# The first loads of q and k, issued ahead of the opening barrier

## The chip, the core and the metric

The kernel runs on one core of a Trainium2 chip. The core has a TensorE (PE), a VectorE (DVE), a ScalarE (ACT), a GpSimd (POOL) and a SyncE (SP), and 16 DMA engines that move data for all of them. SyncE, ScalarE and GpSimd each issue DMA loads into a queue of their own; the queues meet on the same 16 DMA engines. In this text "engine" alone is one of the five, and "DMA engine" is one of the 16.

The metric is the device time of one execution, in microseconds (us). A profile is one traced execution; its span is 1.3 to 1.9 us shorter than the device time of the same execution, so spans are compared with spans and times with times.

## The reference, cut to what matters

```python
# q, k, v: 4 x 6400 x 256 f32; moe_A 8x256x16, moe_B 8x16x256, w_gate 256x8
qn = q / norm(q, axis=1); kn = k / norm(k, axis=1)
a = softmax(kn.T @ qn / tau)             # 256 x 256 for each of 4 batches
x = (v @ a).reshape(25600, 256)
# x + a mixture of 8 low-rank adapters (rank 16), the 2 best of 8 for each row
```

Nothing can be computed before the first rows of q and k are on the chip, and the 256 x 256 product of a batch needs all of that batch's q and k.

## The kernel before: the parts that the change touches

The inputs are f32 in DRAM. Nearly all loads are issued by GpSimd, whose queue casts f32 to bf16 on the way. Only the first 2 of the first batch's 50 row groups of q and k come uncast, over SyncE and ScalarE, and ScalarE casts them; three small MoE loads follow on the same two queues.

```python
def load_consts():                        # called after the first two loads
    ...
    nc.sync.dma_start(W["A0"], ...)       # 128 KB, rows of 512 B
    nc.scalar.dma_start(W["B0"], ...)     # 128 KB, rows of 1 KB
    nc.scalar.dma_start(W["wg0"], ...)    # 8 KB

def do_load(s, what, b, i, c, n):
    ...
        if (b, c) == (0, 0):
            ...
            (nc.sync if what == "q" else nc.scalar).dma_start(W[what], src[b, :, 0:n, :])  # 256 KB each
            return
    nc.gpsimd.dma_start(t[:, c - c0:c - c0 + n, :], src[b, :, c:c + n, :])                  # casts

for s in steps:                           # a static order for all five engines
    do[s.key[0]](s, *s.key[1:])
    if s.key[0] == "load":
        n_load += 1
        if n_load == 2:
            load_consts()
        if n_load == 4:
            make_consts()                 # identity matrix on GpSimd, and others
```

The framework puts an opening barrier ahead of all this. In the built program each of the four other engines executes a DRAIN that counts its arrival up, and then waits for a release. GpSimd writes four small constants, executes a DRAIN, waits until four have arrived, and releases them.

## Time and profile before

| | before |
|---|---|
| device time, 3 runs | 256.03 us median (255.64 to 256.05) |
| span of the profile | 254.1 us |
| busy share: PE, DVE, ACT, POOL | 85%, 75%, 66%, 12% |
| GpSimd's queue (q0), share of 16 DMA engines' span | 74.8% |
| SyncE's queue (q1), share of 16 DMA engines' span | 25.7% |

First from the page of before: the rows of DMA activity in 40 slices of the span (a digit is the busy share in tenths), and the DMA queues with packets, MB and their share of 16 DMA engines' time.

```profile
DMA  7999999999999999999999999999999999999994
...
q0 software_dynamic: 7488, 39.06, 74.8%
q1 hardware_dynamic: 3968, 26.61, 25.7%
q10 hardware_dynamic: 336, 0.40, 0.6%
```

Only the first and the last slice leave the DMA engines time. So the DMA engines are read as the bound, and what is to be had at the start is their idle time. (The page's chain that ended last lies 49% on PE and 39% on DMA, so this reading rests on the DMA row and not on that chain.) The next view is the table of stretches for before: the stretch in us, its length, the busy time of the five engines, the granted clock, the DMA share (over 1 where packets overlap) and GB/s.

```profile
1.00:1.50 0.50, 0.00 (x0) 0.00 (x0) 0.29 (x3) 0.00 (x0) 0.26 (x1) 1.00 0.00 0
1.50:2.00 0.50, 0.00 (x0) 0.00 (x0) 0.00 (x0) 0.00 (x0) 0.50 (x2) 1.00 0.63 66
2.00:2.50 0.50, 0.00 (x0) 0.00 (x0) 0.00 (x0) 0.35 (x1) 0.50 (x2) 1.00 0.86 115
...
4.50:5.00 0.50, 0.00 (x0) 0.00 (x0) 0.00 (x0) 0.38 (x1) 0.50 (x2) 1.00 1.60 306
```

No byte moves before 1.5 us. The timeline of before shows what the engines do meanwhile: start and length in us, engine (SPq, ACTq: the issue of a load), line, operation, tiles, and in brackets the idle time before it and what ended it.

```profile
0.74 0.40 ACTq L540 DMA_DIRECT2D y<-in_k_dram  x1
0.75 0.38 SPq L540 DMA_DIRECT2D y<-in_q_dram  x1
...
1.24 0.66 POOL L542 DMA_DIRECT2D qk<-in_q_dram  x1 [0.79 <-POOLq L925]
...
4.62 1.14 ACT L737 CAST qk<-y 128x512 bf16<-128x512 f32 x2 [0.97 <-DMA y<-in_q_dram]
...
14.72 0.39 PE L557 MATMUL acc_107<-qk 128*128 128x256 bf16 x1 [7.88 <-DMA qk<-in_k_dram]
```

SyncE and ScalarE issue their loads at 0.75 us, as soon as the barrier opens. PE computes on these first rows at 5.8 us and then waits 7.9 us, until 14.72 us, for GpSimd's first k load. So the early rows do not shorten PE's wait themselves; what counts is when GpSimd's stream runs.

### The profile page before, as it was taken

How to read it: one execution, taken by the hardware profiler on the slowest of the kernel's cores; microseconds unless marked ns; L12 is line 12 of the kernel's file. 1: busy time of each engine (PE TensorE's matmuls, PEld its weight loads, DVE VectorE, ACT ScalarE, POOL GpSimd, SP SyncE). 2: the span in 40 equal slices, each digit the busy share in tenths (PEclk: the TensorE clock that was granted, in tenths of full speed). 3: DMA queues.
4: the chain of work that ended last, by engine and by line, in shares of the span. 5: the costliest groups of instructions: out<-in, count | busy, mean ns of one | idle time of the engine just before them, and what ended most of it. 6: DMA issues, size and time to landing. Idle time of an engine off the chain costs nothing.

```text
span 254.1 us, 6344 instructions
## 1 busy us (share of the span) xinstructions
PE 216.1 (85%) x2643; PEld 192.7 (76%) x2643; DVE 190.0 (75%) x486; ACT 166.8 (66%) x270; POOL 30.1 (12%) x58
## 2 busy tenths in 40 slices
PE   0064993899999999999989999879999979999970
PEld 0053881588999996799779999769999869999860
DVE  0055589779889977898979995689888888888910
ACT  4344437558786767888758668453877869768770
POOL 7001220040020002000030100510000210000000
PEclk9999799799999999999999999999999999999997
DMA  7999999999999999999999999999999999999994
GB/s 186 218 215 210 210 221 211 211 220 218 211 219 208 316 299 290 259 213 224 208 214 218 221 212 216 213 208 347 282 282 320 332 323 313 319 421 426 426 411 189
DMA packets 11820, 66.47 MB, mean 262 GB/s; under 512 B 1424, under 2 KB 2320, under 8 KB 7184
## 3 DMA queue, kind: packets, MB, share of 16 engines
q0 software_dynamic: 7488, 39.06, 74.8%
q1 hardware_dynamic: 3968, 26.61, 25.7%
q10 hardware_dynamic: 336, 0.40, 0.6%
q8 instruction: 20, 0.33, 0.5%
q14 instruction: 8, 0.07, 0.1%
HBM read 78.91 MB, written 26.21 MB: 414 GB/s over the span
## 4 chain that ended last, share of the span: by engine, by line
PE 49%; DMA 39%; ACT 3%; DVE 3%; POOL 2%; issue 1%; ACTq 0%; POOLq 0%
DMA qk<-in_k_dram 22%; PE Y_ps L876 13%; DMA v<-in_v_dram 9%; DMA qk<-in_q_dram 8%; PE Y_ps L880 6%; PE T_ps L752 6%; PE ZL_ps L774 4%; PE gzT_ps L863 3%; PE Z_ps L843 2%; PE acc_417 L557 2%; PE acc_418 L557 2%; DVE a_bf L726 2%; PE acc_2620 L557 1%; PE acc_2621 L557 1%; ACT a_exp L678 1%
## 5 line engine op out<-in xcount | busy, mean ns | idle before, releaser
L585 DVE TENSOR_TENSOR ssq<-ssq,sq 128x1280 f32<-128x1280 f32 (+1 forms) x27 | 43.4, 1607 | 27.2 <-ACT sq L579 25.3
L876 PE MATMUL Y_ps<-a_bf,vT 128*128 128x256 bf16 x400 | 60.0, 273 | 0.0
L579 ACT ACTIVATE sq<-qk 128x1280 f32<-128x1280 bf16 (+1 forms) x27 | 36.8, 1364 | 26.5 <-DVE ssq L585 19.7
L732 ACT COPY y<-Y_ps 128x512 f32<-128x512 f32 x79 | 45.8, 587 | 12.3 <-PE Y_ps L880 9.8
L557 PEld LDWEIGHTS <-qk 128*128 128x128 bf16 x400 | 33.8, 103 | 24.5 <-DMA qk<-in_k_dram 16.0
L732 ACT COPY vT<-T_ps 128x1024 bf16<-128x1024 bf16 (+1 forms) x44 | 37.0, 871 | 6.7 <-PE T_ps L752 6.5
L876 PEld LDWEIGHTS <-vT 128*128 128x128 bf16 x400 | 37.6, 98 | 3.7
L880 PE MATMUL Y_ps<-ball,gzT 128*128 128x256 bf16 x200 | 38.2, 273 | 0.3 <-DVE gzT L734 0.3
L557 PE MATMUL acc_107<-qk 128*128 128x256 bf16 x50 | 15.2, 314 | 17.1 <-DMA qk<-in_k_dram 11.3
L542 POOL DMA_DIRECT2D v<-in_v_dram x20 | 12.2, 611 | 128.5 <-PE T_ps L752 80.8
L752 PE MATMUL T_ps<-ident,v 128*128 128x128 bf16 x400 | 27.1, 220 | 0.3 <-DMA v<-in_v_dram 0.3
L561 PEld LDWEIGHTS <-qk 128*128 128x128 bf16 x242 | 24.5, 101 | 3.6
L752 PEld LDWEIGHTS <-v 128*128 128x128 bf16 x400 | 23.9, 98 | 1.5 <-DMA v<-in_v_dram 1.2
L880 PEld LDWEIGHTS <-gzT 128*128 128x128 bf16 x200 | 19.4, 98 | 3.0 <-DVE gzT L734 0.6
L774 PE MATMUL ZL_ps<-waA_sb,vT 128*128 128x136 bf16 x280 | 19.7, 222 | 1.1 <-DVE waA_sb L720 0.9
L863 PE MATMUL gzT_ps<-ident,gz 128*128 128x128 bf16 x200 | 19.7, 219 | 0.3
L734 DVE COPY gzT<-gzT_ps 128x512 bf16<-128x512 bf16 (+1 forms) x39 | 15.0, 390 | 5.7 <-PE gzT_ps L863 5.0
L774 PEld LDWEIGHTS <-vT 128*128 128x128 bf16 x280 | 17.7, 98 | 1.8 <-issue 1.5
L579 ACT ACTIVATE ssq<-qk 128x1536 f32<-128x1536 bf16 x8 | 11.9, 1482 | 9.8 <-DMA qk<-in_k_dram 5.1
L734 DVE COPY y<-Y_ps 128x512 f32<-128x512 f32 x21 | 14.3, 690 | 3.3 <-PE Y_ps L880 3.2
L732 ACT COPY zl<-ZL_ps 128x272 f32<-128x272 f32 (+1 forms) x35 | 13.9, 447 | 3.4 <-PE ZL_ps L774 3.3
L566 PEld LDWEIGHTS <-qk 128*128 128x128 bf16 x168 | 15.2, 100 | 1.2 <-issue 0.2
(304 smaller groups left out, 441.7 us busy)
## 6 DMA issues: line engine op xcount, KB each, us to landing
out_dram<-y SPq DMA_DIRECT2D x18, 1280.0 KB, 18.0
v<-in_v_dram POOLq DMA_DIRECT2D x20, 640.0 KB, 20.5
qk<-in_q_dram POOLq DMA_DIRECT2D x7, 1088.0 KB, 24.1
qk<-in_k_dram POOLq DMA_DIRECT2D x7, 1088.0 KB, 29.0
qk<-in_q_dram POOLq DMA_DIRECT2D x2, 1024.0 KB, 18.8
qk<-in_k_dram POOLq DMA_DIRECT2D x2, 1024.0 KB, 23.2
out_dram<-y SPq DMA_DIRECT2D x4, 512.0 KB, 7.1
qk<-in_q_dram POOLq DMA_DIRECT2D x2, 512.0 KB, 17.3
```

The lines of the kernel that those rows point to most:

```text
L557: nc.tensor.matmul(acc[ic][:, 0:256], kt[:, j, ic * P:(ic + 1) * P], qt[:, j, :], start=c == 0, stop=False, skip_group_check=True)
L561: nc.tensor.matmul(acc[ic][:, 256:384], kt[:, j, ic * P:(ic + 1) * P], kt[:, j, ic * P:(ic + 1) * P], start=False, stop=False, skip_group_ ...
L566: nc.tensor.matmul(acc[ic][:, 384:512], qt[:, j, ic * P:(ic + 1) * P], qt[:, j, ic * P:(ic + 1) * P], start=False, stop=c == NC - 1, skip_ ...
L579: nc.scalar.activation(out[:, 0:n, :], t[:, j:j + n, :], ACT.Square)
L585: nc.vector.tensor_tensor(out=t, in0=t, in1=held["sq", (w, b, g), ""][:, 0:n, :], op=OP.add)
L732: nc.scalar.copy(out, in_)
L734: nc.vector.tensor_copy(out, in_)
L752: nc.tensor.matmul(ps[:, ic, j, :], vt[:, c + j, ic * P:(ic + 1) * P], W["ident"], is_transpose=True, start=(ic + j == 0), stop=(ic == CC ...
L774: nc.tensor.matmul(ps[:, j, :], vT[:, ic, c + j, :], st[b]["waA"][:, ic, :], start=(j == 0 and ic == 0), stop=(j == n - 1 and ic == CC - 1 ...
L863: nc.tensor.matmul(ps[:, j, :], gz[:, j, :], W["ident"], is_transpose=True, start=(j == 0), stop=(j == n - 1))
L876: nc.tensor.matmul(ps[:, j, :], vT[:, ic, c + j, :], st[b]["a"][:, ic, :], start=(j == 0 and ic == 0), stop=False, skip_group_check=True)
L880: nc.tensor.matmul(ps[:, j, :], gzT[:, c + j - UNITS[u][0], :], W["B"], start=False, stop=(j == 1), skip_group_check=True)
```

## The change

Its intent: SyncE and ScalarE have nothing to do while they wait at the barrier, so they issue their first loads ahead of it. GpSimd's loads stay behind it.

```diff
+def first_ahead(nc, names):
+    def move(nc):
+        main, body = nc.main_func.blocks[:2]
+        first = [i for i in body.instructions if i.name in names]
+        ...
+        at = next(n for n, i in enumerate(main.instructions) if type(i).__name__ == "InstMemset")
+        main.instructions = main.instructions[:at] + first + main.instructions[at:]
+        body.instructions = rest
+    nc.at_finalize(move)
 ...
-                (nc.sync if what == "q" else nc.scalar).dma_start(W[what], src[b, :, 0:n, :])
+                early.append((nc.sync if what == "q" else nc.scalar).dma_start(W[what], src[b, :, 0:n, :]))
 ...
+    early = []
 ...
+    first_ahead(nc, {i.ins.name for i in early})
```

In the built program the two loads now stand in front of their engine's DRAIN, that is, in front of its arrival at the barrier.

More of the change, by code (lines that the diff above doesn't have):

```diff
@@ L424 @@
         (2, 4), (3, 2), (3, 4)}
+def first_ahead(nc, names):
+    def move(nc):
+        main, body = nc.main_func.blocks[:2]
+        first = [i for i in body.instructions if i.name in names]
+        assert len(first) == len(names), (names, len(first))
+        rest = [i for i in body.instructions if i.name not in names]
+        at = next(n for n, i in enumerate(main.instructions) if type(i).__name__ == "InstMemset")
+        main.instructions = main.instructions[:at] + first + main.instructions[at:]
+        body.instructions = rest
+    nc.at_finalize(move)
 @with_exitstack
```

## The prediction

> **What bounds the kernel now.** The core's DMA engines. The page's DMA row reads 9 in all slices but the first and last. The table of stretches gives a DMA share of 1.04 for 2-220 us and 0.96 for 220-252 us, against PE busy 0.85 of the span. The only empty DMA time is the start: share 0.00 before 1.5 us, 0.63 in 1.5-2, 0.8 in 2-3.
>
> **What the change moves.** Two issues, q on SyncE (starts at 0.75 us, 0.38 us long) and k on ScalarE (0.74 us, 0.40 us), 256 KB each. Nothing is added or removed. In the trace SyncE arrives at the barrier at 0.00 us and ScalarE at 0.14 us, then both wait for GpSimd's release at 0.63 us. So q should start near 0.0 us and k near 0.14 us: 0.6 to 0.75 us earlier. The MoE loads after them move up by about 0.4 us.
>
> **Cost.** ScalarE reaches the barrier only after its issue: 0.14 plus the 0.43 us between two of its issues is 0.57 us. GpSimd now passes the gathering wait at 0.55 us, so the barrier may open 0.03 to 0.07 us later, and GpSimd's first load (1.24 us) with it.
>
> **How much is worth something.** The trace's DMA packets say that the first bytes of q and k move 1.0 us after issue (1.76 us), and that packets of SyncE's and ScalarE's queues fill the engines until about 5.0 us. GpSimd's queue starts its first packet at 4.35 us and is never empty again until 223 us. The Trainium skill, "DMA: Bandwidth & Descriptors", section "Issuing engines are not separate DMA queues", says that all issuers run on the same 16 engines and interleave; the trace agrees (share up to 1.60 where they overlap, 4.5-5 us). Two cases:
> - GpSimd's queue is held back until 4.35 us by the other queues' packets: it starts up to 0.65 us earlier, and everything shifts by that.
> - Its start is set by GpSimd's own issue: it stays at 4.35 us (or 4.40), but finds the engines nearly free. The other queues' packets after 4.35 us keep 16 engines busy for about 0.5 us (estimate from the packets); this is saved, less the later barrier.
>
> Either way 0.4 to 0.65 us. As the DMA engines never idle afterwards, most of it should reach the end. The earlier casts (ScalarE at 4.62 to about 4.0 us) and first four matmuls (5.81 to about 5.1 us) are worth nothing by themselves: PE then waits for a k load until 14.72 us.
>
> **Prediction.** 255.5 us, range 255.0 to 256.0, against 256.03 before (whose runs scatter by 0.4 us). Faster by over 2%: 0.01; within 2%: 0.98; slower by over 2%: 0.01.
>
> **What would show it.** Timeline: q and k issues before 0.2 us, ScalarE's casts at about 4.0 us, first matmul at about 5.1 us. Stretches: DMA share over 0.5 in 1.0-1.5 us, and below 1.3 in 4.5-5 us. GpSimd's first issue at 1.24 to 1.31 us; k landing that lets PE go on at 14.1 to 14.3 instead of 14.72 us; the same lead (0.3 to 0.7 us) at the last store.
>
> **What would make it wrong.** An issue ahead of the barrier takes longer there, and delays the barrier by more than 0.1 us; the reported time starts with the first issue instead of at a fixed point; DMA engines idle between the early loads and GpSimd's first packet; a matmul clock step (cold until 18.96 us) or a later collision of loads and stores that falls differently.

## The result, and the profile after

| | before | after |
|---|---|---|
| device time | 255.81 us median of 6 (255.64 to 256.05) | 255.69 us median of 6 (255.41 to 256.10) |
| ratio after/before | | 0.9994, 95% interval 0.9981 to 1.0007 |
| same kernel again, second set | 255.72 (11 runs) | 255.20 (6 runs), ratio 0.9978 (0.9963 to 0.9992) |
| same kernel again, third set | 255.84 (11 runs) | 255.52 (5 runs), ratio 0.9985 (0.9973 to 0.9997) |
| span of the first profile | 254.1 us | 254.3 us |

A ratio is the mean time of one kernel's runs over that of the other's of the same rounds, so it is not quite the ratio of the medians that stand beside it. The mean of the three ratios is 0.9986: about 0.36 us faster. The traces are not typical of this. The traced executions of the changed kernel were the slowest of its first set (256.10 us), the second slowest of six in the second (255.54 us) and the slowest of the third (255.75 us); of before, the first trace is of the fourth fastest of six (255.84 us), and that of a later repeat of the fastest of five (255.41 us). So the traced spans have the changed kernel 0.17 us slower on the mean (254.01 against 253.84 us), while the runs have it faster. Traces show where time goes; the gain is read from the runs.

In the DMA row of after's page one digit has changed, that of the first slice:

```profile
DMA  9999999999999999999999999999999999999994
...
q0 software_dynamic: 7488, 39.06, 74.9%
q1 hardware_dynamic: 3968, 26.61, 25.7%
q10 hardware_dynamic: 336, 0.40, 0.5%
```

The stretches of after:

```profile
1.00:1.50 0.50, 0.00 (x0) 0.00 (x0) 0.45 (x3) 0.00 (x0) 0.08 (x1) 1.00 1.24 135
1.50:2.00 0.50, 0.00 (x0) 0.00 (x0) 0.00 (x0) 0.19 (x1) 0.50 (x1) 1.00 0.42 123
2.00:2.50 0.50, 0.00 (x0) 0.00 (x0) 0.00 (x0) 0.50 (x1) 0.50 (x2) 1.00 0.99 381
...
4.50:5.00 0.50, 0.19 (x1) 0.13 (x2) 0.00 (x0) 0.26 (x1) 0.50 (x2) 1.00 0.68 139
```

And the timeline of after:

```profile
0.00 0.38 SPq L554 DMA_DIRECT2D y<-in_q_dram  x1
0.12 0.38 ACTq L554 DMA_DIRECT2D y<-in_k_dram  x1
...
1.42 0.66 POOL L556 DMA_DIRECT2D qk<-in_q_dram  x1 [0.97 <-POOLq L941]
...
3.21 0.60 ACT L751 CAST qk<-y 128x512 bf16<-128x512 f32 x1
4.14 0.62 ACT L751 CAST qk<-y 128x512 bf16<-128x512 f32 x1 [0.33 <-DMA y<-in_k_dram]
...
15.06 2.32 PE L571 MATMUL acc<-qk 128*128 128x256 bf16 x10 [9.21 <-DMA qk<-in_k_dram]
```

Everything early is earlier: the issues by 0.62 and 0.75 us, the data in 1.0 to 1.5 us, the first cast by 1.4 us. Then comes the surprise: PE goes on at 15.06 us instead of 14.72, that is 0.34 us *later*. A second trace of the unchanged kernel (r_before, below) shows how much of this is chance:

```profile
15.15 0.82 PE L557 MATMUL acc<-qk 128*128 128x256 bf16 x3 [7.96 <-DMA qk<-in_k_dram]
```

So before goes on at 14.72 or 15.15 us, and the changed kernel, in its three traces, at 15.06, 14.93 and 15.13 us. What is shown is that the early lead is missing at this point, not that the change makes it later.

To see why, one must look below the load. A load is complete when all 16 DMA engines have counted its semaphore up. The Trainium skill says so in "DMA: Bandwidth & Descriptors", section "Why a DMA increments its semaphore by 16 and not by 1": only the full 16 means that all data landed. The trace agrees; it records each of the 16 increments. Here they are for GpSimd's first load (q, 960 KB), in us, sorted:

```
before  9.32  9.46  9.52  9.55  9.60  9.62  9.62  9.71  9.75  9.77  9.81  9.83  9.94  9.95 10.11 10.13   mean 9.73
after   8.78  8.83  8.85  8.96  9.05  9.08  9.18  9.20  9.41  9.48  9.51  9.63 10.07 10.13 10.29 10.46   mean 9.43
```

The average DMA engine is 0.30 us earlier, which is what the change was to bring. The slowest is 0.33 us later, and the load is complete only with the slowest. The spread over the 16 went from 0.8 us (1.1 us in r_before) to 1.7 us. It also stays: in the same two traces the sixth load (29.9 us) lands 0.25 us earlier on the average and 0.33 us later on the slowest, and the last store 0.09 us earlier on the average and 0.25 us later on the slowest. The trace doesn't name a packet's DMA engine, but each packet can be followed to the one that starts as it ends: in after, the DMA engine whose first load ends last (10.12 us) also ends the second load last (14.69 us).

### The profile page after: what moved, and what is told of

Read it like the earlier page. It is cut to its first block, busy times and chain, and to the rows that moved or that the text cites. A ratio compares the mean times of both kernels' runs of the same rounds, so it can differ in the third digit from the quotient of the medians.

```text
span 254.3 us, 6342 instructions
## 1 busy us (share of the span) xinstructions
PE 215.6 (85%) x2641; PEld 192.6 (76%) x2643; DVE 190.2 (75%) x486; ACT 167.2 (66%) x270; POOL 30.0 (12%) x58
## 4 chain that ended last, share of the span: by engine, by line
PE 49%; DMA 39%; ACT 3%; DVE 3%; POOL 2%; issue 1%; ACTq 0%; POOLq 0%
DMA qk<-in_k_dram 22%; PE Y_ps L890 13%; DMA v<-in_v_dram 9%; DMA qk<-in_q_dram 8%; PE acc L571 7%; PE Y_ps L894 6%; PE T_ps L766 6%; PE ZL_ps L788 4%; PE gzT_ps L877 3%; PE acc L580 2%; PE acc L575 2%; PE Z_ps L857 2%; DVE a_bf L740 2%; ACT a_exp L692 1%; PE log_ps L803 1%
## 5 line engine op out<-in xcount | busy, mean ns | idle before, releaser
L571 PE MATMUL acc<-qk 128*128 128x256 bf16 x400 | 71.0, 286 | 21.0 <-DMA qk<-in_k_dram 15.7
L571 PEld LDWEIGHTS <-qk 128*128 128x128 bf16 x400 | 33.9, 103 | 25.0 <-DMA qk<-in_k_dram 17.4
L575 PE MATMUL acc<-qk 128*128 128x128 bf16 x242 | 34.4, 225 | 0.0
L575 PEld LDWEIGHTS <-qk 128*128 128x128 bf16 x242 | 24.5, 101 | 3.6
L866 DVE TENSOR_TENSOR gz<-zl,gateg 128x512 bf16<-128x512 f32 (+1 forms) x42 | 23.5, 597 | 0.3
L580 PE MATMUL acc<-qk 128*128 128x128 bf16 x168 | 23.7, 224 | 0.0
```

The lines of the kernel that those rows point to most:

```text
L571: nc.tensor.matmul(acc[ic][:, 0:256], kt[:, j, ic * P:(ic + 1) * P], qt[:, j, :], start=c == 0, stop=False, skip_group_check=True)
L575: nc.tensor.matmul(acc[ic][:, 256:384], kt[:, j, ic * P:(ic + 1) * P], kt[:, j, ic * P:(ic + 1) * P], start=False, stop=False, skip_group_ ...
L580: nc.tensor.matmul(acc[ic][:, 384:512], qt[:, j, ic * P:(ic + 1) * P], qt[:, j, ic * P:(ic + 1) * P], start=False, stop=c == NC - 1, skip_ ...
L866: nc.vector.tensor_tensor(out=gz.rearrange("p c (e r) -> p c e r", e=E), in0=z.rearrange("p c (e r) -> p c e r", e=E), in1=held["gate", (b ...
```

## The experiments

Theories for why the gain is smaller and less certain than the 0.75 us of earlier issue:

- **Barrier theory.** The barrier opens 0.17 us later (0.80 instead of 0.63 us), and GpSimd's loads with it.
- **Late-engine theory.** The lead is real for the average DMA engine, but a load counts on its slowest one, and the early start makes the 16 less even, and the late one stays late.
- For the unevenness itself, an **early-queue** (or overlap) theory: GpSimd's first packets run among the other queues' packets and suffer from it.

One more reading of the traces is used throughout. GpSimd's first two loads are 256 packets of 7,680 bytes. An undisturbed one takes 0.587 us. "Slow" are those over 0.62 us; "lost" is their time over 0.587 us, summed and divided by 16, so in us for an average DMA engine. Landings are average/slowest of the 16 DMA engines; the last column is the time of all runs of that set, with the ratio to before in the same rounds.

| kernel | GpSimd: first issue, first packet | slow packets, lost | first load lands | sixth load lands | span | time; ratio (95%) |
|---|---|---|---|---|---|---|
| before | 1.24, 4.35 | 0, 0.00 | 9.73/10.13 | 29.54/29.93 | 254.05 | 255.81 |
| r_before | 1.24, 4.49 | 0, 0.00 | 9.74/10.55 | 29.56/30.36 | 253.63 | 255.62; 0.9992 (0.9980 to 1.0004) |
| after | 1.42, 3.63 | 28, 0.40 | 9.43/10.46 | 29.29/30.26 | 254.29 | 255.69; 0.9994 |
| r_after | 1.43, 3.72 | 21, 0.24 | 9.27/10.34 | 29.08/30.13 | 253.76 | 255.20; 0.9978 |
| r_after2 | 1.42, 3.71 | 25, 0.39 | 9.38/10.55 | 29.20/30.32 | 253.97 | 255.52; 0.9985 |
| e_arrive_first | 1.23, 3.86 | 40, 0.78 | 10.03/10.58 | 29.85/30.38 | 254.36 | 255.94; 1.0000 (0.9985 to 1.0016) |
| e_pool_ahead | 0.73, 2.69 | 37, 0.32 | 8.22/10.66 | 34.68/37.12 | 259.94 | 261.25; 1.0215 (1.0202 to 1.0229) |
| e_pool_after_drain | 1.06, 3.06 | 40, 0.81 | 10.10/11.48 | 30.28/31.65 | 255.67 | 256.76; 1.0043 (1.0024 to 1.0061) |
| e_q_only | 1.29, 3.39 | 31, 0.40 | 9.45/11.55 | 29.35/31.41 | 255.59 | 257.00; 1.0030 (1.0008 to 1.0053) |
| e_const_late | 1.41, 3.05 | 27, 0.65 | 9.11/10.08 | 29.97/30.91 | 255.59 | 257.39; 1.0057 (1.0032 to 1.0082) |
| e_ident_first | 1.60, 3.69 | 27, 0.34 | 9.35/10.49 | 29.18/30.30 | 253.64 | 255.45; 0.9990 (0.9970 to 1.0009) |
| e_all_hw_ahead | 1.24, 3.99 | 38, 0.54 | 9.98/11.03 | 29.83/30.82 | 254.36 | 256.27; 1.0023 (1.0007 to 1.0040) |
| e_all_ident | 1.43, 3.81 | 19, 0.27 | 9.47/10.68 | 29.28/30.48 | 253.78 | 256.33; 1.0018 (1.0005 to 1.0031) |
| e_pool_later | 2.64, 4.02 | 20, 0.71 | 9.88/10.50 | 29.69/30.30 | 254.10 | 255.95; 1.0017 (1.0003 to 1.0030) |

All kernels gave the right result.

### r_before, r_after, r_after2: the same kernels again

No edit.

> The kernel before, once more, as a null test and for a second profile. Both theories: ratio 1.000 within 0.0015. Its first GpSimd load should again land on all 16 DMA engines between about 9.3 and 10.1 us. If that last landing moves by more than 0.3 us with nothing changed, the scatter of the start is as large as what the change is worth.

> The changed kernel, once more. In its first profile the first GpSimd load landed 0.30 us earlier on the mean DMA engine but 0.33 us later on the slowest (10.46 against 10.13 us), and that difference stayed to the end. Late-engine theory (a load counts when its slowest engine has landed, and an engine that starts late stays late, as all are saturated): the slowest landing varies from profile to profile, and the span follows it within 0.2 us. Barrier theory (the barrier opens 0.17 us later and takes GpSimd's loads with it): the slowest landing is again 0.2 to 0.35 us later than in the repeat of before. Time 255.4 to 255.9 in both.

> The changed kernel a third time, beside the experiments of this call. Two earlier sets gave 255.69 and 255.20 us against 255.8 and 255.7 us of before. If the lead is real and its size a matter of how the 16 DMA engines start, this set lies at 255.1 to 255.8 us, its runs scatter more than before's (0.7 to 1.1 us against 0.4 to 0.9 us from lowest to highest), and the first GpSimd load lands on average 0.3 to 0.5 us earlier than before's 9.74 us, on the slowest engine anywhere from 9.8 to 10.6 us.

The null test gave 0.9992, so a ratio of 0.999 from one such set is noise. The slowest landing of before's first load moved from 10.13 to 10.55 us with nothing changed, more than the 0.3 us that the expectation set as a warning, and yet that execution was the shorter one (span 253.63 against 254.05 us). So before is not free of a late DMA engine either, and in that pair the first load alone does not order the spans: by the eighth load (34 us) the repeat was already 0.04 us ahead on the slowest DMA engine.

r_after's expectation put a test to the late-engine theory: the span should follow the slowest landing within 0.2 us. It failed. From after to r_after the slowest landing moved by -0.12 us and the span by -0.53 us; to r_after2 by +0.09 and -0.32 us. The time, 255.20 us, also fell below the 255.4 to 255.9 us expected. r_after2 met its expectation in full (255.52 us, runs 0.72 us apart, first load 0.36 us earlier on the average, 10.55 us on the slowest).

What does repeat is the rest. Three traces of the changed kernel have 21 to 28 slow packets, two of before have none. The average landing leads by 0.30 to 0.47 us in all three. The slowest lands at 10.34 to 10.55 us, against 10.13 and 10.55 us in before: no lead. The changed kernel's 17 runs lie between 254.71 and 256.10 us; the 28 runs of before in the same rounds lie between 255.46 and 256.35 us. The barrier theory, which wanted the slowest to be 0.2 to 0.35 us later than in the repeat of before each time, fails here already: it was 0.21 us earlier and equal.

### e_arrive_first: arrive, then issue, then wait

```diff
-        main.instructions = main.instructions[:at] + first + main.instructions[at:]
+        for i in main.instructions:
+            out.append(i)
+            if type(i).__name__ == "InstDrain":
+                out += [x for x in first if x.engine == i.engine]
+        main.instructions = out
```

> SyncE and ScalarE first arrive at the barrier, then issue their loads while they wait for its release. The loads go out as early as in the changed kernel (0.05 and 0.17 us), and the barrier should open at 0.63 us as before, GpSimd's first issue be back at about 1.24 us. Barrier theory: the 0.17 us come back, the first GpSimd load lands at 10.1 us or sooner, time 0.2 to 0.4 us under the changed kernel (255.2 to 255.5). Late-engine theory: no fixed gain from that; the time stays within 0.2 us of the changed kernel (255.5 to 255.9), with the spread of landings (0.8 before, 1.7 us changed) deciding.

The barrier part came out as planned: released at 0.62 us, GpSimd's first issue at 1.23 us, q and k still early (0.09 and 0.21 us). The gain did not come: 255.94 us, ratio 1.0000, while the changed kernel had 0.9978 in the same rounds. With 40 slow packets and 0.78 us lost, the average landing (10.03 us) fell behind before's. Giving back the barrier's 0.17 us brought nothing, so the barrier theory has no support; as the edit also brought more slow packets, it is not a clean measure of those 0.17 us alone. The late-engine theory missed too: it wanted the time within 0.2 us of the changed kernel's, and it was 0.74 us longer.

### e_pool_ahead: GpSimd's first two loads ahead of the barrier too

```diff
-        nc.gpsimd.dma_start(t[:, c - c0:c - c0 + n, :], src[b, :, c:c + n, :])
+        load = nc.gpsimd.dma_start(t[:, c - c0:c - c0 + n, :], src[b, :, c:c + n, :])
+        if what != "v" and (b, i) == (0, 0):
+            early.append(load)
```

> The changed kernel with GpSimd's first q and k loads also ahead of the barrier: issued at about 0.15 and 0.8 us instead of 1.42 and 2.08 us; the barrier then opens at about 1.6 us. If GpSimd's issue time is what the start waits for (barrier theory), the first GpSimd packet comes about 1.2 us earlier, the load lands at 9.0 to 9.4 us, time 0.8 to 1.2 us under the changed kernel. If the engines are busy with the other queues' packets anyway (late-engine theory), the gain is only what idle engine time is filled: 0.2 to 0.7 us, time 255.0 to 255.5.

Both theories missed: 5.5 us slower. The timeline of this kernel says why:

```profile
1.39 0.54 POOL L556 DMA_DIRECT2D qk<-in_k_dram  x1
...
2.01 0.13 POOL L943 MEMSET const-uint8-127<- 128x1 uint8 x1
15.86 0.20 POOL masks.py:197 MEMSET ident<- 128x128 bf16 x1 [13.72 <-POOLq L943]
16.14 0.29 POOL masks.py:199 TENSOR_SCALAR_AFFINE_SELECT ident<-ident 128x128 bf16<-128x128 bf16 x1
16.48 0.55 POOL L556 DMA_DIRECT2D qk<-in_q_dram  x1
```

GpSimd stands still for 13.7 us. In the trace its DRAIN at the barrier lasts 14.37 us, from 1.25 to 15.62 us; in before it lasts 0.19 us. The second of the two loads landed on its slowest DMA engine at 15.49 us. So a DRAIN on GpSimd that follows loads ended only when they had landed, while the DRAINs of SyncE and ScalarE behind a load lasted 0.12 and 0.14 us. The third GpSimd load then went out at 16.5 instead of 3.0 us. The second stretch of idle DMA time cost far more than the first could give. This is why GpSimd's loads must stay behind the barrier, or at least behind that DRAIN.

Its start also shows the late DMA engine at its clearest: 15 of 16 land the first load by 8.65 us, the last at 10.66 us. That one took its first GpSimd packet at 5.32 us, the others at 2.69 to 3.23 us. Why, no run shows.

### e_pool_after_drain: the same, but behind GpSimd's DRAIN

```diff
+            if type(i).__name__ == "InstDrain" and i.engine == mybir.EngineType.Pool:
+                out += pool        # its first q and k load
```

> The changed kernel with GpSimd's first two loads ahead of its wait at the barrier, but behind its DRAIN. In the run with both in front of that DRAIN, it lasted 14.4 us, until the two loads had landed, and the kernel took 5.5 us more. If the DRAIN is the cause: it lasts 0.2 us again, GpSimd's first issue starts at about 1.1 us, the barrier opens at about 2.2 us, the MoE loads follow at 2.3 us, and the 5.5 us are gone: 254.9 to 255.7 us. If something else about an early GpSimd load is at fault (the barrier's lateness, the collision of the queues), the time stays over 257 us.

The DRAIN lasted 0.19 us again and 4.5 of the 5.5 us were gone, so the DRAIN was the cause. But 256.76 us is still about 0.9 us slower than before, though GpSimd's first packet came 1.3 us sooner (3.06 us). The MoE loads were issued at 1.67 to 2.07 us here (0.92 to 1.31 in the changed kernel), so that they met GpSimd's stream on the DMA engines. Their time to landing shows it: the last of them landed at 16.4 us, against 5.7 us or less in the three traces of the changed kernel.

In before's trace the packets of the three MoE loads occupy 1.10 us of each DMA engine on average. Before and after, most of this is spent before GpSimd's stream is under way: of these 264 KB, at most 89 KB (before) and 50 to 78 KB (after) were still to go at its first packet. Here all of them were, and the stream is about 0.7 us later by the sixth load (30.28 against 29.54 us), in spite of its earlier start. The slow packets count too: an estimate from these numbers is 1.3 us of earlier start, less 1.10 us of MoE packets and 0.81 us lost, which makes 0.6 us later.

### e_q_only: q ahead, k behind

```diff
-                early.append((nc.sync if what == "q" else nc.scalar).dma_start(...))
+                load = (nc.sync if what == "q" else nc.scalar).dma_start(...)
+                if what == "q":
+                    early.append(load)
```

> Only SyncE's q load goes ahead of the barrier; k is issued by ScalarE after it, as before. The barrier should open at about 0.66 us, as SyncE's DRAIN ends at about 0.56 us. If the lead is simply earlier engine time, half of the early bytes give about half of it: mean landing of the first GpSimd load 0.1 to 0.3 us earlier than before, time 255.3 to 255.7 us. If the later barrier (0.17 us) had eaten a fixed part of the gain, this one would do as well as or better than the whole change (under 255.3 us).

This run separates average from slowest. The average landing led before's by 0.28 us, as expected. But the six runs were 257.37, 256.94, 257.07, 257.11, 255.46 and 255.69 us. The profiled one was the slowest, and its increments of the first load show one straggler:

```
before    ...  9.94  9.95 10.11 10.13
e_q_only  ...  9.79  9.87  9.97 11.55
```

The straggler also has the last MoE packets. From the DMA issues of e_q_only (queue that issued it, count, KB, us from issue to landing):

```profile
y<-in_moe_A_dram SPq DMA_DIRECT2D x1, 128.0 KB, 4.2
y<-in_moe_B_dram ACTq DMA_DIRECT2D x1, 128.0 KB, 9.1
y<-in_moe_w_gate_dram ACTq DMA_DIRECT2D x1, 8.0 KB, 10.0
```

In after the same three read:

```profile
y<-in_moe_B_dram ACTq DMA_DIRECT2D x1, 128.0 KB, 4.3
y<-in_moe_A_dram SPq DMA_DIRECT2D x1, 128.0 KB, 4.1
y<-in_moe_w_gate_dram ACTq DMA_DIRECT2D x1, 8.0 KB, 4.4
```

GpSimd's queue started at 3.39 us, when 192 KB of the other queues were still to go (50 to 78 KB in the three traces of the changed kernel). The last MoE B packet went at 9.45 us (5.11 us in before). The Trainium skill, "DMA: Bandwidth & Descriptors", section "Queues, rings and completion order", says that each DMA engine "round-robins between the queue rows it has work for, at *packet* granularity". The trace agrees: followed packet by packet, the straggler alternates MoE B packets of 59 ns with GpSimd packets of 587 ns, so that five of the former are spread from 6.96 to 9.45 us.

But this taking of turns explains why MoE B landed late, and little of why the straggler did: those five packets and the gate load's add about 0.3 us. Its eight GpSimd packets run from 5.61 to 11.25 us; at 4.8 us the other 15 DMA engines each had one under way. Its first one took 1.37 us. So it started late and slowly, as in e_pool_ahead, and again no run shows why.

The late DMA engine then stayed late. At the sixth load the average is 0.19 us ahead of before and the slowest 1.48 us behind; the span is 1.54 us longer. Here, with a straggler of 1.5 us, it follows the slowest.

The two runs at 255.5 and 255.7 us fit an execution without such a straggler, but only the profiled one has a trace, so that is inferred.

### e_const_late: the MoE loads after 10 us

```diff
-            if n_load == 2:
-                load_consts()
             if n_load == 4:
                 make_consts()
+                nc.sync.dma_start(scrap, held["qk", ("q", 0, 0), ""][0:1, QK[0][1] - 1, 0:16])  # waits for the load
+                load_consts()            # all three on SyncE
```

> The changed kernel, with the three MoE loads taken out of the start: SyncE issues them after the first GpSimd q load has landed (about 10 us). Overlap theory (the first GpSimd packets are slow and uneven because they run among the small packets of the MoE loads, all within 3.5 to 5 us): GpSimd's first packets then all take 0.59 us, the spread of the first landing falls to 0.8 us or less, its slowest engine lands by 9.5 us, and the time goes to 254.7 to 255.2 us. Rival (the slow packets have another cause, or the engine time is only moved): spread stays over 1.2 us, or comes back at 10 to 12 us with the moved loads, and the time stays within 0.25 us of the changed kernel of this call.

The overlap theory fails on its own ground: with no MoE packet near, there are still 27 slow packets, 0.65 us lost, and the spread stays at 1.6 us. The rest of its prediction fails too: 257.39 us. The rival's time (within 0.25 us of the changed kernel's 255.52 us) was missed as well. The average lead of 0.62 us at the first load became a lag of 0.43 us at the sixth. The difference, 1.05 us, is about the MoE loads' own 1.10 us of DMA engine time, now paid inside the stream. The extra wait and ScalarE's two saved issues are changed too, but no wait that they touch was found to matter; that was not tested apart.

### e_ident_first, e_all_hw_ahead, e_all_ident, e_pool_later: when GpSimd's queue starts

```diff
 # e_ident_first: the identity matrix before GpSimd's first load
             if n_load == 2:
                 load_consts()
-            if n_load == 4:
                 make_consts()
 # e_all_hw_ahead: e_arrive_first, with the MoE loads moved as well
-        nc.sync.dma_start(W["A0"], ...)
+        early.append(nc.sync.dma_start(W["A0"], ...))     # the same for B0 and wg0
 # e_all_ident: both
 # e_pool_later: e_ident_first, and
+        for _ in range(4):
+            nc.gpsimd.memset(ident, 0.0)
```

> The changed kernel, with GpSimd building the identity matrix (0.55 us) before its first two loads, so these are issued at about 2.0 us instead of 1.42. In all profiles with early loads, 21 to 40 of the 256 packets of GpSimd's first two loads took over 0.62 us instead of 0.587 (0.24 to 0.81 us lost on the average engine); in both profiles of before, none. Early-queue theory (they are slow because GpSimd's queue starts moving while the engines still have the other loads' packets, or its own descriptors are fresh): with the first packet at 4.2 us or later the slow packets are gone (under 5), the first load's mean landing stays at 9.3 to 9.5 us although it was issued 0.55 us later, and the slowest lands under 10.1 us; time 255.0 to 255.5 us. Rival (the slow packets belong to the start of that queue whatever the time, or to the early loads as such): over 15 slow packets again, and the mean landing goes to 9.8 to 10.0 us; time 255.8 to 256.3 us.

> All five loads of SyncE and ScalarE (q, k and the three MoE loads) are issued after the engine has arrived at the barrier and before it waits for the release. GpSimd's first issue is back at 1.24 us. Early-queue theory: the other queues' packets are done about 0.3 us sooner than in the changed kernel (by 4.7 us at the latest), but GpSimd's queue starts sooner too; slow packets stay (15 to 40), time 255.3 to 256.0 us. Rival (only the loads' own lateness counts): first load on average at 9.1 us or sooner, time 254.8 to 255.2 us.

> Both: all five loads of SyncE and ScalarE between arrival and release, and GpSimd's identity matrix before its first loads (issue at about 1.8 us). Early-queue theory: the other queues are nearly done (4.5 us) when GpSimd's first packet comes at about 4.0 to 4.2 us; few slow packets (under 8), first load on average at 9.1 to 9.3 us, slowest under 9.9 us, time 254.8 to 255.4 us: the best of all. Rival: as slow as the changed kernel or slower, 255.5 to 256.2 us.

> The changed kernel, with GpSimd's identity matrix and four idle fills of the same tile ahead of its first two loads. In the run with the matrix alone in front, the first issue moved from 1.42 to only 1.60 us (most of it ran in time that the engine needed for its first load anyway), so that GpSimd's first packet stayed at 3.7 us. Now the issue should start at 2.4 to 2.7 us and the first packet come at 4.3 to 4.9 us, when the other queues are done (4.4 to 4.7 us) or nearly. Early-queue theory: under 5 slow packets of 256; the first load lands on average at 9.4 to 9.8 us in spite of an issue over 1 us later, with a spread of 0.9 us or less; time 255.2 to 255.9 us. Rival (slow packets belong to every start with early loads): 15 or more again, first load on average at 9.9 us or later, time 256.0 us or more.

e_ident_first did not do what it was built for: GpSimd took 0.62 us between the release and its first issue without the matrix too (before and after), and the matrix ran in that time, so the issue moved by only 0.18 us. It equals the changed kernel within the noise. e_all_hw_ahead and e_all_ident are slower than before by a clear, small amount: more loads ahead of the release is not better. Neither did what was expected: e_all_hw_ahead came out 0.3 us above its range, and e_all_ident, expected to be the best of all with under 8 slow packets, had 19 and came out above its rival's range too. e_all_ident's profile (span 253.78 us) is from its fastest run, which should warn a reader against judging it by that trace.

e_pool_later did delay the queue, to a first packet at 4.02 us. The early-queue theory wanted the slow packets gone. There were 20, and they came in one burst: nearly all of the loss (11.2 of 11.3 us summed over the 16) from packets that started between 4 and 5 us, up to 1.62 us long. Most of these still started beside the other queues' last packets (18 KB, done by 4.42 us), so this run alone does not decide. Two other traces do. In before, 89 KB of the other queues were still to go at GpSimd's first packet, 18 of its packets started before MoE A and B were done (5.18 us), and none was slow: overlap is not enough. In e_const_late, 23 of the 27 slow ones started after the last packet of the early q and k (3.24 us) and before the first of the moved MoE loads: overlap is not needed.

The theory's other half, that the queue's own descriptors are fresh, was not tested: from issue to first packet GpSimd's first load took 3.1 and 3.25 us in the two traces of before, and 1.4 to 2.75 us in all twelve others. e_pool_later moved issue and first packet together. The rival wording, that they belong to a start with early loads, fits those twelve traces, but it is a description and not a cause. **What makes GpSimd's first packets slow stays open.**

## Why the prediction was right or wrong

The time was right: 255.5 us predicted, with 255.0 to 256.0; measured 255.69, 255.20 and 255.52 us. That alone says little: before's own median, 255.81 us with six runs, lies in the range too. The gain says more: 0.53 us was forecast, and 0.36 us is the mean of three sets. Of its steps:

- **The bound.** Right as far as the DMA row goes. The DMA engines are busy from 1.8 us (before) or 1.0 us (after) to the last stores, but not fully at the start: the share was 0.77 to 0.86 in 2 to 3 us before, and 0.42 in 1.5 to 2.0 us and 0.68 in 4.5 to 5.0 us after. What these gaps cost was not separated.
- **What moves.** Right. q is issued at 0.00 and k at 0.12 us; the prediction had near 0.0 and near 0.14.
- **The barrier "may open 0.03 to 0.07 us later".** Wrong in size: 0.17 us (0.80 instead of 0.63). The prediction counted ScalarE's issue and forgot that the DRAIN behind a load is not the DRAIN without one: 0.14 us against 0.01 us. GpSimd's first issue came at 1.42 us, outside the 1.24 to 1.31 us it allowed. No run shows that this cost anything.
- **Two cases for GpSimd's queue.** The first was right: its first packet came 0.63 to 0.72 us earlier than 4.35 us although its issue came 0.18 us later. It had been held back by the other queues' packets.
- **"Either way 0.4 to 0.65 us".** This is the term that was too large. The average DMA engine got 0.30 to 0.46 us against before's first trace. The missing part is of the size of the slow packets: 0.24 to 0.40 us lost, zero in before. That these eat the rest of the lead is an estimate from two measured numbers; their cause is open.
- **"As the DMA engines never idle afterwards, most of it should reach the end".** Right over the runs, and unclear in the traces. The gain of the runs, 0.36 us, is as large as the average DMA engine's lead, 0.30 to 0.46 us. In the three traces, which lie at the slow end of their sets, the last store was 0.09 to 0.38 us earlier than in before's first trace on the average DMA engine; on the slowest it was +0.25, -0.28 and -0.07 us, and against the repeat of before it was later in all three. Two and three traces, whose spans differ by 0.4 and 0.5 us within one kernel, don't settle a difference of 0.4 us. What the prediction left out is that a late DMA engine stays late. How much that costs in general is not shown: over 13 profiles (e_pool_ahead left out) the span correlates at 0.86 with the slowest landing of the sixth load and at 0.63 with the average one, but three profiles make the first number, those where MoE loads met the stream (e_pool_after_drain, e_q_only, e_const_late). Over the other ten it is 0.29 with the slowest and 0.63 with the average. So a straggler of over 1 us shows at the end; the smaller unevenness of the changed kernel was not shown to.
- **"k landing that lets PE go on at 14.1 to 14.3".** Wrong: 15.06, 14.93 and 15.13 us, as the slowest DMA engine did not get the lead. It also took one trace's 14.72 us for before, which was 15.15 us in the repeat.
- **The earlier casts and matmuls are worth nothing.** Right: the first cast came at 3.21 us (about 4.0 was expected), the first matmul at 4.81 us (about 5.1), and PE then waited 9.2 us instead of 7.9.
- Of what would make the prediction wrong, it named the barrier (0.17 us came, over its limit of 0.1), an idle gap (the share of 0.42 is one), the clock and later collisions. It did not name unevenness among the 16 DMA engines.

No experiment beat the changed kernel by more than the noise; over its three sets it is about 0.14% faster than before.

## What to carry to other kernels

When the DMA engines bound a kernel from end to end, look at a load's 16 landings and not only at its end: an early start that helps 15 of them and hurts one can be worth less than nothing (e_q_only: 0.28 us earlier on the average, 1.4 us later on the slowest, and 0.8 us slower by the ratio of all its runs). And trace a kernel more than once: two traces of the same kernel differed by 0.4 us here, as much as the change was worth. Use the idle time before the main stream for the small loads, and see that they are done before the stream starts, since small packets that meet it take turns with its large ones. Ahead of a barrier, an issue from SyncE or ScalarE is cheap, but loads on GpSimd must not stand in front of its DRAIN.

## What the Trainium skill lacked or had wrong

- No page says whether loads of its own queue that are still in flight hold up a DRAIN on GpSimd: here it lasted 14.37 us, until both loads had landed, against 0.19 us without. "VectorE: DVE Perf Modes" tells of boilerplate DRAINs of about 12 ns on all five engines; SyncE's and ScalarE's took 0.007 and 0.008 us before, 0.12 and 0.14 us behind a load.
- "DMA: Bandwidth & Descriptors", section "Latency and other measured facts", gives about 600 ns to the first byte for the queues of SyncE and ScalarE and about 1 us for GpSimd's. It does not say from when it counts. Counted from the start of SyncE's issue the first packet took 1.0 us in before and after; counted from its end, 0.63 and 0.62 us, which agrees. For GpSimd's first load it was 1.38 to 3.25 us from the start of the issue, the longest where other queues were full.
- The same page (section "Queues, rings and completion order") explains the round robin, but gives no cost for small loads beside a stream of large packets: 128 KB that landed in 4.3 us before the stream took 9.1 us where it met the stream.
- No page warns that unevenness among the 16 DMA engines persists while all are busy: a spread of 1.7 to 1.8 us at the first load was still 1.6 us at the sixth (the three traces of the changed kernel).
- None explains the slow first packets of GpSimd's queue: none of 256 in before, 19 to 40 in every kernel with early loads, up to 1.73 us instead of 0.587 us.
